# Gated linear attention with an MLP on one core: cosine from the absolute phase, six equal gate units, and a planner that knows a shared port and the order of the loads

## The chip, the cores and the metric

The program runs on one core of a Trainium2 chip. The metric is device time in microseconds (us) of one execution, lower is better. Engines are named as the profile names them: PE (TensorE, matrix products), DVE (VectorE), ACT (ScalarE, function tables), POOL (GpSimd) and SP, which here only issues loads and stores.

## The reference

Four batches, eight heads, 768 steps, 48 channels a head. A complex decay is applied at each step to a 48x48 state of each head; only the real part is read:

```python
mag = np.sqrt(a_re * a_re + a_im * a_im)
scale = np.minimum(mag, 0.999) / (mag + 1e-06)
for t in range(S):
    S_re, S_im = ar * S_re - ai * S_im + kv, ar * S_im + ai * S_re   # kv = k_t (x) v_t
    y[:, :, t] = einsum('bhd,bhde->bhe', q[:, :, t], S_re)
# x = y as [4, 768, 384]; then layer norm without bias, and
out = x + np.maximum(norm(x) * g_ln @ w_ch1, 0) @ w_ch2              # 384 -> 1536 -> 384
```

## The kernel before

The steps are cut into 24 chunks of 128, and the work goes in 12 **pairs** of two chunks, three pairs to a batch. A pair does this, with the planner's names for the steps:

- **Gates.** SP loads `are` and `aim` of the pair. ACT takes `ln` (into `w`) and `iv` (an exponential), DVE multiplies to `r` (the tangent of the phase step), `r2` is its square, ACT takes `u` (a logarithm), DVE makes the log magnitude `l`. PE sums `l` along the steps (`dec`), and ACT makes `e` and `en` from the sums. These ACT steps need the logarithm table.
- **Phase.** With the other table ACT takes the arctangent `th`, PE sums it along the steps (`ph`, in two PSUM banks, read back as 16-bit turns), DVE keeps the end for the next pair (`car`), ACT takes the sine of the phase (`sin`) and of half the phase (`sh`), and POOL or DVE makes the cosine from the latter, as 1 - 2 sh squared (`cos`, two instructions).
- **Attention.** `ke` and `qe` are k and q times the magnitudes, `ks` and `qs` those times cosine and sine (always DVE). PE transposes them, they are copied out of PSUM (`ksT`, `qsT`), PE forms the 128x128 scores (`am`), DVE masks them (`atm`), and PE forms `y`, with the state `G` carried by `gm`. `x` copies `y` out of PSUM.
- **MLP.** Statistics on DVE (`bn`), three transposes (`xtr`, `xT`), `mm1` with `relu` on ACT, `mm2`, and `ot` adds x. SP stores. The first layer's weights are folded once with the layer norm (`wp` on PE, `wc` copies).

Pairs are taken in **units** that share the table loads (`t_log`, `t_trig`) and the chunk decays (`tot`, `et`, `dps`, `decc`): `[[0], [1], [2, 3], [4, 5], [6, 7], [8, 9], [10, 11]]`.

No loop sets the order. Every step is put in a `Graph` with an engine, a cost, its needs and the ring buffers that it uses (k, q and `are` three deep, `vf` two). `Graph.order` is a list planner: at each turn it takes the engine that can start first, and among the steps ready within `SLACK` the one with the lowest key (a number of its group, plus its pair). A step with a second engine in `alt` goes where it would end first. The steps are then emitted in that order, and each engine runs its own in that order. The weights `w1r` and `w2b` are two DMAs issued by POOL (step `wl`), which convert to bf16 on the way; all other loads are SP's. The small constants (`one_b` to `cmat`) are made on POOL at the start.

Of the kernel before, what the change touches and what calls it, by code (L numbers as in the profile page):

```python
# [39 lines left out]
CHUNK = 0.196  # L40
SLACK = {"PE": 0, "ACT": 0.381, "DVE": 0.179, "POOL": 0.515, "SP": 0.565}
# [13 lines left out]
class Graph:  # L55
# [7 lines left out]
    def add(self, name, eng, cost, group, pos, emit, needs=(), uses=(), ps=None, alt=None, tail=0.0, c=0):  # L63
        assert name not in self.ops, name
        alts = {eng: (cost, tail)}
        if alt:
            alts[alt[0]] = (alt[1], tail)
        self.ops[name] = Op(name, alts, group, pos, emit, list(needs), list(uses), ps)
        self.ops[name].c = c

    def order(self, keys):
# [20 lines left out]
        dma_free = 0.0  # L92
# [9 lines left out]
        done = []  # L102
# [83 lines left out]
def kernel(  # L186
# [28 lines left out]
    UNITS = [[0], [1], [2, 3], [4, 5], [6, 7], [8, 9], [10, 11]]  # L215
# [46 lines left out]
    one_b = pool.tile([C, 1], FP32, name="one_b")  # L262
    half_n = pool.tile([C, R], FP32, name="half_n")
# [53 lines left out]
    for i, (f, cost) in enumerate(((c_one, .1), (c_ue, 1.6), (c_ue2, .5), (c_pick, 2.65),  # L317
                                   (c_ident, 1.85), (c_mask, 2.1), (c_sel, .6), (c_cmat, 5.0))):
# [11 lines left out]
    for i in range(2):  # L330
        g.add(("wl", i), "POOL", 1.4, "wl", i, lambda i=i: wl(i), tail=6.7)
# [8 lines left out]
    g.add(("wgc",), "DVE", .7, "wp", -1, wgc, needs=[("c_cmat",), ("gln",)])  # L340
    for jb in range(DF // 512):
        for ec in range(ND):
# [11 lines left out]
            g.add(("wc", jb, ec), "DVE", .6, "wc", jb * .1, wc, needs=[o], ps=(o, 1), alt=("ACT", .49))  # L354
# [14 lines left out]
    def pair_ops(P):  # L369
# [28 lines left out]
        def tt(name, **kw):  # L398
            engine(name).tensor_tensor(**kw)  # L399
# [25 lines left out]
        add(("l", P), "DVE", 1.27, f_l, needs=[("u", P)],  # L425
# [37 lines left out]
        if not last:  # L463
# [248 lines left out]
```

## Time and profile before

| | |
|---|---|
| time, median of 3 runs | 246.85 us (245.52 to 247.14) |
| the profiled execution's own time | 248.44 us |
| its span in the trace | 246.7 us |
| mean granted TensorE clock | 0.985 |
| DMA packets | 105671, 31.00 MB |

The span runs from the first to the last instruction; the 1.74 us beyond it are outside the trace. In the rows below a line such as L399 is a helper's line that many steps share, so steps are told apart by tile names. Buffer numbers are left out in the trace. The copies that write `w1b`, `ksT`, `qsT` share L358 (ACT) and L360 (DVE). The tile of `r2` is written as `r`.

### The profile page before, as it was taken

The numbers are of one execution on the slowest core, as the hardware profiler recorded it, in microseconds if no ns is written. First come the engines' busy times: TensorE is split into PE (matmuls) and PEld (weight loads), VectorE is DVE, ScalarE is ACT, GpSimd is POOL, SyncE is SP. The second block draws the span as 40 slices with busy tenths as digits, with TensorE's granted clock in tenths as the row PEclk, the third lists the DMA queues.
The fourth block names the chain that finished last, engine by engine and source line by source line (L and its number), as shares of the span: only waits on it lengthen the run. The fifth ranks groups of instructions, "written<-read, shape, count | busy, mean of one in ns | idle before, by whom it ended". The sixth has DMA issues, their size and how long they took to land. (4 is left out here: it accounts for less than half of the span.)

```text
span 246.7 us, 5275 instructions
## 1 busy us (share of the span) xinstructions
PE 198.2 (80%) x2123; PEld 147.2 (60%) x2123; DVE 192.3 (78%) x313; ACT 158.3 (64%) x193; POOL 104.0 (42%) x121
## 2 busy tenths in 40 slices
PE   0340087698896999989999878999698999999993
PEld 0020085247575867676677666696565887878762
DVE  0400669399999997999998998899999969996322
ACT  4260455598967769896694985599957857615320
POOL 8700321535966238583446670451675307301100
PEclk9999999799999999999999997999999999999999
DMA  7999898979984455928579044183421000001102
GB/s 194 251 205 196 189 210 170 201 175 291 185 186 111 130 159 112 201 73 192 162 139 217 32 115 111 32 160 100 92 69 35 33 3 35 0 35 35 64 32 96
DMA packets 105671, 31.00 MB, mean 126 GB/s; under 512 B 100656, under 2 KB 105264, under 8 KB 105648
## 3 DMA queue, kind: packets, MB, share of 16 engines
q1 hardware_dynamic: 103696, 28.32, 49.6%
q0 software_dynamic: 1952, 2.36, 5.5%
q8 instruction: 16, 0.26, 0.4%
q14 instruction: 7, 0.06, 0.1%
HBM read 28.31 MB, written 4.72 MB: 134 GB/s over the span
## 5 line engine op out<-in xcount | busy, mean ns | idle before, releaser
L623 PE MATMUL banks<-w2b,h 128*128 128x384 bf16 x288 | 55.6, 330 | 0.2 <-ACT h L614 0.2
L605 PE MATMUL banks<-xT,w1b 128*128 128x256 bf16 x432 | 53.2, 273 | 1.3 <-DVE xT L584 0.6
L605 PEld LDWEIGHTS <-w1b 128*128 128x128 bf16 x432 | 41.1, 98 | 8.7 <-DVE w1b L360 1.2
L614 ACT ACTIVATE h<-banks 128x1024 bf16<-128x1024 f32 x36 | 36.3, 1019 | 10.9 <-PE banks L605 10.8
L623 PEld LDWEIGHTS <-h 128*128 128x128 bf16 x288 | 26.4, 99 | 14.3 <-issue 1.4
L399 DVE TENSOR_TENSOR atm<-banks,mask 128x1024 bf16<-128x1024 f32 x24 | 28.6, 1214 | 3.1 <-PE banks L525 3.1
L507 PE MATMUL banks<-ident,ks 128*96 128x128 bf16 x192 | 14.3, 229 | 20.3 <-DVE ks L399 19.9
L399 POOL TENSOR_TENSOR r<-r 128x768 f16<-128x768 f16 x10 | 17.4, 1745 | 21.9 <-DVE r L399 21.9
L507 PEld LDWEIGHTS <-ks 128*96 128x96 bf16 x192 | 12.8, 129 | 23.1 <-DVE ks L399 22.8
L399 POOL TENSOR_TENSOR ke<-k,en 128x384 bf16<-128x384 f32 x13 | 14.1, 1101 | 27.2 <-ACT en L440 20.5
L569 ACT CAST x<-banks 128x384 bf16<-128x384 f32 x24 | 11.4, 478 | 19.0 <-PE banks L563 14.6
L629 DVE SCALAR_TENSOR_TENSOR ot<-banks,rstd,x 128x384 f32<-128x384 f32 x24 | 14.6, 609 | 10.5 <-PE banks L623 10.3
L476 POOL TENSOR_TENSOR sh<-sh 128x768 f16<-128x768 f16 x10 | 15.9, 1590 | 15.9 <-ACT sh L467 15.9
L399 DVE TENSOR_TENSOR qs<-qe,trig 128x768 bf16<-128x768 bf16 x24 | 21.7, 917 | 0.0
L399 POOL TENSOR_TENSOR qe<-q,e 128x384 bf16<-128x384 f32 x12 | 11.8, 988 | 20.3 <-DMA q<-in_q_dram 16.8
L399 DVE TENSOR_TENSOR ks<-ke,trig 128x768 bf16<-128x768 bf16 x24 | 19.3, 818 | 0.9 <-ACT trig L470 0.9
L435 PE MATMUL banks<-l,u_e 128*128 128x384 f16 x48 | 10.4, 342 | 11.7 <-DVE l L423 11.7
L591 POOL TENSOR_SCALAR rstd<-mv 128x2 f32<-128x2 f32 x12 | 3.4, 283 | 38.1 <-DVE mv L574 36.9
L643 ACT ACT_TABLE_LOAD x14 | 18.0, 1283 | 1.0 <-PEq L696 0.8
L507 PE MATMUL banks<-ident,qs 128*96 128x128 bf16 x192 | 14.2, 228 | 4.2 <-DVE ksT L360 2.3
L470 ACT ACTIVATE trig<-banks 128x768 bf16<-128x768 int16 x12 | 9.8, 816 | 10.6 <-DVE car L464 10.6
L454 PE MATMUL banks<-th,u_th 128*128 128x384 f16 x48 | 13.0, 357 | 4.0 <-ACT th L444 4.0
(78 smaller groups left out, 422.9 us busy)
## 6 DMA issues: line engine op xcount, KB each, us to landing
are<-in_a_re_dram SPq DMA_DIRECT2D x12, 384.0 KB, 3.5
aim<-in_a_im_dram SPq DMA_DIRECT2D x12, 384.0 KB, 4.3
k<-in_k_dram SPq DMA_DIRECT2D x24, 192.0 KB, 3.7
q<-in_q_dram SPq DMA_DIRECT2D x24, 192.0 KB, 3.8
vf<-in_v_dram SPq DMA_DIRECT2D x24, 192.0 KB, 3.6
out_dram<-ot SPq DMA_DIRECT2D x24, 192.0 KB, 1.9
w1r<-in_moe_w_ch_dram POOLq DMA_DIRECT2D x1, 1152.0 KB, 11.1
w2b<-in_moe_w_ch_dram POOLq DMA_DIRECT2D x1, 1152.0 KB, 17.9
```

The costliest lines, as they stand in the source:

```text
L399: engine(name).tensor_tensor(**kw)
L435: nc.tensor.matmul(heads(ps[:, c, 0:DM]), lhsT=u_e[:, c, j], rhs=step(T("l", P), j), start=(j == 0), stop=(j == R - 1))
L454: nc.tensor.matmul(heads(ps[:, c, 0:DM]), lhsT=u_th[:, c, j], rhs=step(T("th", P), j), start=False, stop=(j == R - 1))
L470: add(("sin", P), "ACT", .7, lambda: act(out=T("trig", P)[:, 1], in_=v16(), func=AF.Sin, scale=TWO_PI_SAFE / TURN), needs=[("ph", P)], use ...
L476: eng.tensor_tensor(out=T("sh", P), in0=T("sh", P), in1=T("sh", P), op=ALU.mult)
L507: nc.tensor.transpose(ps[:, h], T(nm, P)[:, c, h].rearrange("p a d -> p (a d)"), ident)
L569: add(("x", n), "ACT", .38, lambda n=n: nc.scalar.copy(out=T("x", n), in_=bank(("y", n))[:, 0:DM]), needs=[("y", n)], uses=[("x", n)], c=c ...
L605: nc.tensor.matmul(ps[:, jj], lhsT=w1b[:, dc, ts(gi * JG + jj, C)], rhs=T("xT", P)[:, dc].rearrange("p c t -> p (c t)"), start=(dc == 0), ...
L614: add(("relu", P, gi), "ACT", .91, lambda gi=gi, o=o: act(out=T("h", P)[:, ts(gi, JG)], in_=bank2(o).rearrange("p s (j t) -> p (s j) t", t ...
L623: nc.tensor.matmul(bank(("o", n))[:, 0:DM], lhsT=T("h", P)[:, j, ts(c, C)], rhs=w2b[:, j], start=(j == 0), stop=(j == NJ - 1))
L629: add(("ot", n), "DVE", .54, lambda n=n, c=c: nc.vector.scalar_tensor_tensor(out=T("ot", n), in0=bank(("o", n))[:, 0:DM], scalar=T("rstd", ...
L643: nc.scalar.preload_act_table_set({"log": "natural_log_exp_and_others", "trig": "trig_and_small"}[name])
```

## The change

The half-angle sine `sh` is replaced by the absolute value of the phase (`abs`, on DVE or ACT, written to the tile `sh`), and the cosine becomes one more ACT step, sin(pi/2 - |phase|), with a bias tile `quarter`. `r2` may run on ACT too, and `x` on DVE too. The first two units of one pair become one unit of two. The planner gets new keys, costs and slacks, a second condition for POOL and DVE steps that are marked `lock` (they don't overlap in its model), a model of how the POOL-issued loads push back the ones in flight, and the weight loads are added to the graph last.

```diff
-KEYS = {"ld_a": -10.982, "ld_qk": -2.438, "ld_v": -1.699, "vcast": 4.3, "t_log": -4.145, "ln":
...
+KEYS = {"const": -19.045, "ld_a": -3.747, "ld_qk": -2.454, "ld_v": -2.007, "vcast": 1.508,
...
+BIAS = {"abs": 0.134, "r2": -0.1, "ke": 0.052, "qe": 0.05, "kT": 0.179, "qT": -0.551, "wc": -1.356, "x": 0.12}
-SLACK = {"PE": 0, "ACT": 0.381, "DVE": 0.179, "POOL": 0.515, "SP": 0.565}
+SLACK = {"PE": 0, "ACT": 0, "DVE": 0, "POOL": 0, "SP": 0.478}
...
+                    if e in ("POOL", "DVE") and op.lock:
+                        t = max(t, lock_free)
...
+            if e in ("POOL", "DVE") and op.lock:
+                lock_free = t + cost
...
-            if tail:
+            if tail and e == "POOL":
+                for o, at in queued:
+                    if at > t:
+                        o.end += tail
+                dma_free = max(dma_free, t + cost) + tail
+                op.end = t + cost + tail + 1.8
+            elif tail:
+                queued.append((op, max(dma_free, t + cost)))
...
-    UNITS = [[0], [1], [2, 3], [4, 5], [6, 7], [8, 9], [10, 11]]
+    UNITS = [[0, 1], [2, 3], [4, 5], [6, 7], [8, 9], [10, 11]]
...
-        add(("r2", P), "POOL", 1.7, lambda: tt(("r2", P), out=flat(T("r2", P)), in0=flat(T("r", P)),
-                                               in1=flat(T("r", P)), op=ALU.mult),
-            needs=[("r", P)], uses=[("r", P), ("r2", P)], alt=("DVE", .48))
+        def f_r2():
+            if g.ops[("r2", P)].eng == "ACT":
+                act(out=flat(T("r2", P)), in_=flat(T("r", P)), func=AF.Square)
+            else:
+                tt(("r2", P), out=flat(T("r2", P)), in0=flat(T("r", P)), in1=flat(T("r", P)), op=ALU.mult)
+        add(("r2", P), "POOL", 1.7, f_r2, needs=[("r", P)], uses=[("r", P), ("r2", P)],
+            alt=[("DVE", .48), ("ACT", .74)], lock=True)
...
-        add(("sh", P), "ACT", .7, lambda: act(out=T("sh", P), in_=v16(), func=AF.Sin,
-                                               scale=TWO_PI_SAFE / TURN / 2),
-            needs=[("ph", P)], uses=[("sh", P)], key="sin", ps=(("ph", P), 2))
+        def f_abs():
+            if g.ops[("abs", P)].eng == "ACT":
+                act(out=T("sh", P), in_=v16(), func=AF.Abs)
+            else:
+                nc.vector.tensor_reduce(out=T("sh", P), in_=v16().unsqueeze(3), op=ALU.max,
+                                        axis=mybir.AxisListType.X, apply_absolute_value=True)
+        add(("abs", P), "DVE", .88, f_abs, alt=[("ACT", .7)], needs=[("ph", P)], uses=[("sh", P)], ps=(("ph", P), 2))
...
-        def f_cos():
-            eng = engine(("cos", P))
-            eng.tensor_tensor(out=T("sh", P), in0=T("sh", P), in1=T("sh", P), op=ALU.mult)
-            eng.tensor_scalar(out=T("trig", P)[:, 0], in0=T("sh", P), scalar1=-2.0, scalar2=1.0,
-                              op0=ALU.mult, op1=ALU.add)
-        add(("cos", P), "POOL", 2.5, f_cos, needs=[("sh", P)], uses=[("sh", P), ("trig", P)],
-            alt=("DVE", .9))
+        add(("cos", P), "ACT", .83, lambda: act(out=T("trig", P)[:, 0], in_=T("sh", P), func=AF.Sin,
+                                                scale=-TWO_PI_SAFE / TURN, bias=quarter),
+            needs=[("abs", P), ("c_one",)], uses=[("sh", P), ("trig", P)])
...
-            add(("x", n), "ACT", .38, lambda n=n: nc.scalar.copy(out=T("x", n), in_=bank(("y", n))[:, 0:DM]),
-                needs=[("y", n)], uses=[("x", n)], c=c, ps=(("y", n), 1))
+            add(("x", n), "ACT", .38, lambda n=n: put(("x", n), T("x", n), bank(("y", n))[:, 0:DM]),
+                alt=[("DVE", .47)], needs=[("y", n)], uses=[("x", n)], c=c, ps=(("y", n), 1))
```

What this makes of the instructions, counted over the whole program: on POOL the ten pairs of cosine instructions and ten of the `r2` squares go, and `ke`/`qe` rise from 25 to 30. On DVE come six `abs`, twelve `x` and five more `r2`; two cosines (two instructions each), six `w1b` copies, two copies of `ksT`/`qsT` in all and five `ke`/`qe` go. On ACT come twelve `cos`, five squares, six `w1b` copies and two `ksT`/`qsT` copies in all; six of the twelve `sh` passes stay as `abs`; twelve `x`, two table loads and one `et` go. PE loses sixteen small products.

POOL at the start, before: the two weight DMAs stand ahead of `sel` and `cmat`.

```order
masks.py:65 MEMSET mask 128x128
masks.py:66 AFFINE_SELECT mask<-mask 128x128
L326 DMA w1r<-in_moe_w_ch_dram 128x3x1536
L304 MEMSET sel 128x8
L307 MEMSET sel 64x1 x4
L308 MEMSET half_n 128x2
L328 DMA w2b<-in_moe_w_ch_dram 128x12x384
L311 MEMSET cmat 128x1152
L313 AFFINE_SELECT cmat<-cmat 128x384 x3
```

POOL at the start, now:

```order
masks.py:65 MEMSET mask 128x128
masks.py:66 AFFINE_SELECT mask<-mask 128x128
L323 MEMSET sel 128x8
L326 MEMSET sel 64x1 x4
L327 MEMSET half_n 128x2
L330 MEMSET cmat 128x1152
L332 AFFINE_SELECT cmat<-cmat 128x384 x3
L345 DMA w1r<-in_moe_w_ch_dram 128x3x1536
L347 DMA w2b<-in_moe_w_ch_dram 128x12x384
```

Both weight loads are issued after every constant. SP's loads at the start, before (`are_64` is the first ring buffer of `are`, and so on):

```order
L378 DMA are_64<-in_a_re_dram 128x8x96
L378 DMA aim_67<-in_a_im_dram 128x8x96
L378 DMA are_65<-in_a_re_dram 128x8x96
L378 DMA aim_68<-in_a_im_dram 128x8x96
L378 DMA are_66<-in_a_re_dram 128x8x96
L378 DMA aim_69<-in_a_im_dram 128x8x96
L383 DMA k_73<-in_k_dram 128x8x48
L383 DMA q_70<-in_q_dram 128x8x48
```

SP's loads at the start, now:

```order
L395 DMA are_65<-in_a_re_dram 128x8x96
L395 DMA aim_68<-in_a_im_dram 128x8x96
L400 DMA k_73<-in_k_dram 128x8x48
L400 DMA q_70<-in_q_dram 128x8x48
L400 DMA k_73<-in_k_dram 128x8x48
L400 DMA q_70<-in_q_dram 128x8x48
L404 DMA vf_76<-in_v_dram 128x8x48
L349 DMA gln<-in_moe_g_ln_dram 128x3x1
L404 DMA vf_76<-in_v_dram 128x8x48
L395 DMA are_66<-in_a_re_dram 128x8x96
```

The third pair's gates now stand behind the first pair's k, q and v. ACT's first phase, before: one pair's gates, the table, one pair's sines, and the other table.

```order
L440 ACTIVATE e_99<-banks 128x768
L643 ACT_TABLE_LOAD
L444 ACTIVATE th_92<-r_84 128x768
L467 ACTIVATE sh_106<-banks 128x768
L470 ACTIVATE trig_103<-banks 128x768
L643 ACT_TABLE_LOAD
L405 ACTIVATE w_83<-are_65 128x768
```

ACT's first phase, now (`trig_103` and `trig_104` are the first two pairs'):

```order
L684 ACTIVATE et_94<-banks 4x768
L663 ACT_TABLE_LOAD
L465 ACTIVATE th_92<-r_84 128x768
L465 ACTIVATE th_93<-r_85 128x768
L495 ACTIVATE trig_103<-banks 128x768
L498 ACTIVATE trig_103<-sh_106,quarter 128x768
L490 ACTIVATE sh_107<-banks 128x768
L495 ACTIVATE trig_104<-banks 128x768
L498 ACTIVATE trig_104<-sh_107,quarter 128x768
L663 ACT_TABLE_LOAD
```

Both pairs pass through one visit to each table; the first pair's `abs` is not in ACT's list, it stands in DVE's.

## Rows read from the trace of the kernel before

**Rows 1.** By stretch: length; busy PE, PEld, DVE, ACT, POOL; clock, DMA share, GB/s.
```profile
0.00:8.00 8.00, 0.00 (x0) 0.10 (x1) 1.81 (x3) 3.32 (x4) 6.80 (x27) 1.00 0.82 221
8.00:25.00 17.00, 5.16 (x20) 1.90 (x19) 1.67 (x3) 5.74 (x7) 2.89 (x4) 1.00 1.17 206
25.00:48.00 23.00, 12.58 (x118) 9.56 (x119) 15.31 (x30) 12.69 (x15) 6.42 (x8) 0.93 0.94 192
48.00:57.00 9.00, 7.82 (x44) 3.99 (x43) 8.94 (x13) 8.18 (x11) 5.07 (x4) 0.99 0.79 187
57.00:220.00 163.00, 149.65 (x1724) 114.69 (x1725) 153.79 (x244) 120.97 (x149) 80.94 (x77) 0.99 0.48 111
220.00:246.70 26.70, 23.03 (x224) 16.94 (x222) 10.83 (x23) 7.44 (x9) 1.84 (x4) 0.99 0.15 55
```

**Rows 2.** Timeline of the start: start, duration, instruction, [idle before it, releaser].
```profile
4.25 0.84 ACT L405 ACTIVATE w<-are 128x768 f32<-128x768 f32 x1 [2.18 <-DMA are<-in_a_re_dram]
...
5.11 1.00 POOL L326 DMA_DIRECT2D w1r<-in_moe_w_ch_dram  x1
...
6.90 1.06 POOL L328 DMA_DIRECT2D w2b<-in_moe_w_ch_dram  x1
6.94 6.65 SPq L383 DMA_DIRECT2D k<-in_k_dram  x1
...
9.10 1.87 POOL L313 TENSOR_SCALAR_AFFINE_SELECT cmat<-cmat 128x384 f16<-128x384 f16 x3
...
13.91 1.28 ACT L643 ACT_TABLE_LOAD   x1
...
17.90 0.81 ACT L467 ACTIVATE sh<-banks 128x768 f16<-128x768 int16 x1 [1.85 <-PE banks L454]
...
25.39 0.56 DVE L399 TENSOR_TENSOR ke<-k,en 128x384 bf16<-128x384 f32 x1 [11.13 <-DMA k<-in_k_dram]
...
31.89 1.94 PE L507 MATMUL banks<-ident,ks 128*96 128x128 bf16 x16 [14.03 <-DVE ks L399]
...
33.88 0.69 DVE L360 COPY ksT<-banks 96x1024 bf16<-96x1024 bf16 x1 [0.70 <-PE banks L507]
```

**Rows 3.** First two loads of `aim`, by tile, and time from issue to landing.
```profile
L378 SPq DMA_DIRECT2D aim<-in_a_im_dram x2: 567/858/1150, 1.3 to 3.0; - x2
...
DMA to landing us min/median/max: 4.1/4.6/5.2
```

**Rows 4.** First two loads of `k`, by tile, and time from issue to landing.
```profile
L383 SPq DMA_DIRECT2D k<-in_k_dram x2: 4139/5394/6648, 6.9 to 19.0; - x2
...
DMA to landing us min/median/max: 7.8/13.1/18.4
```

**Rows 5.** The page's DMA issues: size, us from issue to landing.
```profile
w2b<-in_moe_w_ch_dram POOLq DMA_DIRECT2D x1, 1152.0 KB, 17.9
```

**Rows 6.** The page's costliest groups: count, busy us, mean ns, idle before and releaser.
```profile
L399 DVE TENSOR_TENSOR atm<-banks,mask 128x1024 bf16<-128x1024 f32 x24 | 28.6, 1214 | 3.1 <-PE banks L525 3.1
...
L399 POOL TENSOR_TENSOR r<-r 128x768 f16<-128x768 f16 x10 | 17.4, 1745 | 21.9 <-DVE r L399 21.9
...
L569 ACT CAST x<-banks 128x384 bf16<-128x384 f32 x24 | 11.4, 478 | 19.0 <-PE banks L563 14.6
...
L476 POOL TENSOR_TENSOR sh<-sh 128x768 f16<-128x768 f16 x10 | 15.9, 1590 | 15.9 <-ACT sh L467 15.9
L399 DVE TENSOR_TENSOR qs<-qe,trig 128x768 bf16<-128x768 bf16 x24 | 21.7, 917 | 0.0
...
L399 DVE TENSOR_TENSOR ks<-ke,trig 128x768 bf16<-128x768 bf16 x24 | 19.3, 818 | 0.9 <-ACT trig L470 0.9
...
L470 ACT ACTIVATE trig<-banks 128x768 bf16<-128x768 int16 x12 | 9.8, 816 | 10.6 <-DVE car L464 10.6
```

**Rows 7.** Groups by form: the cosine's second instruction on POOL.
```profile
L477 POOL TENSOR_SCALAR trig<-sh 128x768 bf16<-128x768 f16 x10 | 9.6, 962 | 0.9
```

**Rows 8.** By tile: least, median and longest ns of `ks` on DVE.
```profile
L399 DVE TENSOR_TENSOR ks<-ke,trig x24: 526/568/1815, 28.8 to 212.0; 128x768 bf16<-128x768 bf16 x24
```

More of the change, by code (lines that the diff above doesn't have):

```diff
@@ L61, in __init__, with add @@
         self.bank = {}
-    def add(self, name, eng, cost, group, pos, emit, needs=(), uses=(), ps=None, alt=None, tail=0.0, c=0):
+    def add(self, name, eng, cost, group, pos, emit, needs=(), uses=(), ps=None, alt=None, tail=0.0, c=0, lock=False):
         assert name not in self.ops, name
         alts = {eng: (cost, tail)}
-        if alt:
-            alts[alt[0]] = (alt[1], tail)
+        for e, c_ in alt or ():
+            alts[e] = (c_, tail)
         self.ops[name] = Op(name, alts, group, pos, emit, list(needs), list(uses), ps)
         self.ops[name].c = c
+        self.ops[name].lock = lock
     def order(self, keys):
@@ L101, in order @@
                     ready[e].append(op)
-        done = []
+        done, queued = [], []
         def choose(n):
@@ L135, in order @@
                         t = max(t, b[0])
+                    if e in ("POOL", "DVE") and op.lock:
+                        t = max(t, lock_free)
                     if len(op.alts) > 1:
-                        other = [x for x in op.alts if x != e][0]
-                        if free[other] + op.alts[other][0] < t + op.alts[e][0] - 0.01:
+                        main = next(iter(op.alts))
+                        end = t + op.alts[e][0] + (BIAS[op.group] if e != main else 0.0)
+                        if any(max(free[x], t if x == "POOL" else 0.0) + op.alts[x][0]
+                               + (BIAS[op.group] if x != main else 0.0) < end - 0.01
+                               for x in op.alts if x != e):
                             continue
@@ L272, in c_one @@
         nc.gpsimd.memset(one_b, 1.0)
+        nc.gpsimd.memset(quarter, PI / 2)
     def c_ue():
@@ L338, in wgc @@
                                     scalar2=None, op0=ALU.mult)
-    g.add(("wgc",), "DVE", .7, "wp", -1, wgc, needs=[("c_cmat",), ("gln",)])
+    g.add(("wgc",), "DVE", .7, "wp", -.1, wgc, needs=[("c_cmat",), ("gln",)])
     for jb in range(DF // 512):
@@ L353 @@
             g.add(o, "PE", .66, "wp", jb * .1, wp, needs=[("wgc",), ("wl", 0)], ps=(o, 1))
-            g.add(("wc", jb, ec), "DVE", .6, "wc", jb * .1, wc, needs=[o], ps=(o, 1), alt=("ACT", .49))
+            g.add(("wc", jb, ec), "DVE", .6, "wc", jb * .1, wc, needs=[o], ps=(o, 1), alt=[("ACT", .49)])
     def put(name, dst, src):
@@ L424, in f_l @@
                                     scalar2=LNEPS, op0=ALU.min, op1=ALU.add)
-        add(("l", P), "DVE", 1.27, f_l, needs=[("u", P)],
+        add(("l", P), "DVE", 1.27, f_l, lock=True, needs=[("u", P)],
             uses=[("r2", P), ("w", P), ("l", P)])
@@ L511, in f_cp @@
                 put(name, T(dst, n), bank(o, D2).bitcast(BF16).rearrange("p (h t) -> p h t", h=H))
[L513 to L514 removed]
+            for nm, src, eng, alt in (("kT", "ks", ("DVE", .61), [("ACT", .91)]),
+                                      ("qT", "qs", ("ACT", .91), [("DVE", .61)])):
                 o = (nm, n)
@@ L593, in f_rstd @@
             nc.gpsimd.tensor_tensor(out=t, in0=t, in1=half_n, op=ALU.pow)
-        add(("rstd", P), "POOL", 1.0, f_rstd, needs=[("bn", P * R), ("bn", P * R + 1), ("c_sel",)],
+        add(("rstd", P), "POOL", 1.0, f_rstd, lock=True, needs=[("bn", P * R), ("bn", P * R + 1), ("c_sel",)],
             uses=[("mv", P), ("rstd", P)])
@@ L646 @@
     for ui, us in enumerate(UNITS):
-        before = [] if ui == 0 else [(nm, P) for P in UNITS[ui - 1] for nm in ("th", "sin", "sh")]
-        g.add(("t_log", ui), "ACT", 1.28, "t_log", us[0], lambda: table("log"), needs=before)
+        before = [] if ui == 0 else [(nm, P) for P in UNITS[ui - 1] for nm in ("th", "sin", "cos")]
+        g.add(("t_log", ui), "ACT", 1.3, "t_log", us[0], lambda: table("log"), needs=before)
         logs = [(nm, P) for P in us for nm in ("ln", "iv", "u", "e", "en")] + [("et", ui)]
-        g.add(("t_trig", ui), "ACT", 1.28, "t_trig", us[0], lambda: table("trig"), needs=logs)
+        g.add(("t_trig", ui), "ACT", 1.3, "t_trig", us[0], lambda: table("trig"), needs=logs)
         rows = 2 * len(us)
@@ L679 @@
             needs=[("dps", ui)], uses=[("dec", ui)], ps=(("dps", ui), 1))
+    for i in range(2):
+        g.add(("wl", i), "POOL", 1.4, "wl", i, lambda i=i: wl(i), tail=(6.2, 7.7)[i])
     for op in g.order(KEYS):
```

42 lines of the change are left out of this document (20 added, 22 removed), and 10 rows, old and new, of the table KEYS.

## Prediction

> **What bounds the kernel now.** I read the busy time by stretch first, since an average over the span hides the start. From 57 to 220 us PE is busy 149.65 of 163 us (92%) and DVE 153.79 (94%), so two engines are nearly full there and no single wait is worth much; ACT has 42 us idle and POOL half its time [rows 1]. After 220 us PE is busy 23.03 of 26.7: the last pairs' MLP. The start is different. In the 17 us from 8 to 25 PE is busy 5.16, DVE 1.67 and ACT 5.74, while the DMA engines are fully busy (share above 1) [rows 1]. The timeline says what is waited for. DVE stands idle 11.13 us until the first half of k lands, and `ke` starts at 25.39; PE gets its first transposes at 31.89 [rows 2]. That half of k was handed to the queue at 6.94, took 6.65 us to be accepted [rows 2] and landed 18.4 us after the start of its issue, at 25.3 [rows 4]. The second weight load, issued at 6.90 [rows 2], landed 17.9 us later, at 24.8 [rows 5]. Before the weights flowed, loads came fast: the second `aim`, issued at 3.04, landed 5.2 us later, at 8.2, and the first, issued at 1.29, at 5.4 [rows 3]: two 384 KB loads in 2.8 us, 1.4 each. So the weight loads, which nobody needs before the first layer's folding, starve the first k and q.
>
> **The start, step by step.** Weights: `sel` and `cmat` now stand ahead. The stretch from the end of the first weight issue, 6.11, to the end of `cmat`, 9.10 + 1.87 = 10.97, holds these constants and one weight issue of 1.06, so they take 3.8 us, and the first weight issue moves from 5.11 to about 9.0 [rows 2]. The old one began at 5.11 and the second `aim` still landed undisturbed at 8.2, so the squeeze begins some 3 us after the issue starts: now at about 12.
>
> Loads: two pairs' gates land by 8.2 as before. Then k, q, k, q of pair 0 instead of a third pair's gates. Once the weights were through, the first two halves of k landed at 25.3 and 18.96 + 7.8 = 26.8 with one q between [rows 4], 0.75 us apiece. Four of them are there by 8.2 + 4 x 0.75 = 11.2 at best, by 8.2 + 4 x 1.4 = 13.8 if each takes as long as a gate load; I take 12, because they are half the size. What comes behind them (v of pair 0, the third pair's gates) goes through the squeeze, which lasts as long as before and ends near 12 + 16.6 = 28.6 instead of 24.8. That v is needed only for `gm` and `y`, the gates only for the next unit.
>
> Gates of two pairs: before, the first load was used at 4.25 and the table switched at 13.91 [rows 2]. One pair more on ACT is five passes of about 0.84 (the `w` pass [rows 2]), 4.2 us; in series with DVE and PE as the first pair's were, it would be 9.66. Much of the second pair fits into ACT's waits for the first, but its `u` and `e` each queue behind one of them, so I take 5.1: table at 19.0. From the table to the first phase pass took 17.90 - 13.91 = 4.0, so the first `sin` is at 23.0. `sin`, `abs` and `cos` follow one another: 0.81, 0.91 and 0.81 to 25.5. (`abs` has no row; by columns it is 768/1024 of `atm`'s 1214 ns, 0.91, between `ks`'s least, 0.53 on the same columns, and `atm`'s 1.21, more columns and two inputs [rows 6, 8].) Sine and cosine products on two DVE halves, 0.55 each, put the first whole `qs` at 27.0, where PE had its first transposes at 31.89: 4.9 us earlier.
>
> Pair 1 gains more, because it no longer waits for a second round of both tables. I count by DVE, which then runs through. Before, DVE had done 1.81 + 1.67 + 15.31 + 8.94 = 27.73 us of work by 57.0 [rows 1]. In the changed list the work up to the second `xT` of pair 0 is 46 rows: 17 products and squares at 0.56 [rows 2], three `r` and three `l`, 7.1, two `atm`, 2.4 [rows 6], four copies at 0.69 [rows 2], `abs` and two `car`, 2.0, and small ones, 4.0: 27.8 us, as much. Of it 10.0 lies ahead of the first products of pair 0, so 17.8 follow from 25.3 on, and I add 1.6 of waits (the cold transposes, 1.94 for sixteen [rows 2], and `u` behind the weight copies on ACT): 44.7. **The lead is 57.0 - 44.7 = 12.3 us.** It counts only if loads keep up: by 57 us both kernels have moved the same bytes, since the DMA engines were busy all along (shares 0.94 and 0.79 from 25 to 57 [rows 1]).
>
> **The rest, step by step.** POOL loses 17.4 + 15.9 + 9.6 = 42.9 us of squares and cosines [rows 6, 7] and gains five products near 1.05, so of its 94.3 us after 25 us [rows 1] 40% go. This matters to DVE: `ks` takes 526 ns at least, 568 in the median, 1815 at worst [rows 8], 818 in the mean, `qs` 917 [rows 6]. Above the least that is 24 x 0.29 + 24 x 0.39 = 16.4 us; 40% less is 6.6 us saved.
> The Trainium skill, page "SBUF — State Buffer", section "SBUF: two separate sides", says that DVE and GpSimd share one port pair under an exclusive lock and that the loser fully blocks. The longest `ks` agrees; by that rule alone the whole 16.4 could go if nothing overlapped, which is the third case below.
>
> DVE gains six `abs`, 5.5 (3.2 to 7.3), twelve `x` at ACT's 0.48 [rows 6], 5.7, five squares at 0.53, 2.7; it loses six weight copies (0.64, by columns of `x`), 3.8, two cosines, 2.1, five `ke`/`qe` at 0.56, 2.8, two PSUM copies, 1.2: +4.0 net. DVE ends 2.6 us lighter (0.8 to 4.9). ACT: six passes more for the cosine (twelve `cos`, six `sh` gone), 4.9; five squares, 4.2; copies of weights and `ksT`/`qsT`, some 5; less twelve `x`, 5.7, two tables of 1.28 and an `et`: 5 us more, covered by its 42 us of idle time; without that cover they would cost 5. PE's sixteen small products cost nothing either way. PE has 163 - 149.65 = 13.35 us of idle time in the long stretch as a ceiling to any gain there, so DVE's 2.6 can be cashed; I take **2.6** (0 to 5). The last 26.7 us keep their form, mm1 and mm2 of the last pair.
>
> Sum: 12.3 + 2.6 = 14.9 us. The profiled run was 248.44 (span 246.7), which gives 233.5; against the median, 246.85, it is **232.0**.
>
> **Rivals.**
> *The squeeze catches pair 0 after all.* If the eighth load isn't through by 12, it lands when the weights are done, near 29, `qe` follows, and as that product stands in DVE's queue ahead of `abs`, the first products come at 31.0 instead of 25.3: 5.7 us of the lead go, 232.0 + 5.7 = 237.7. For it: the margin is under a microsecond, and SP was held 6.65 us by a full queue [rows 2]. Against: that hold began only when weights were flowing.
> The Trainium skill, page "DMA: Bandwidth & Descriptors", section "Queues, rings and completion order", says that each DMA engine takes turns between queues by packet; the k that took 18.4 us agrees, and by that rule weights don't wait for loads issued earlier.
>
> *The port relief is worth all of it.* With POOL's long instructions gone and the rest kept apart, DVE saves 16.4 - 4.0 = 12.4, within PE's 13.35: 246.85 - 12.3 - 12.4 = 222.2. Against: thirty POOL products remain, and PE is at 92% already.
>
> *The cosine stops ACT, slower.* In four units a `cos` on ACT waits for an `abs` that stands in DVE's queue, with `relu` behind it on ACT and PE behind that. `sin` already lost 10.6 us waiting for `car` on DVE [rows 6]. An `abs` behind two `atm` makes 2 x 1.21 + 0.91 = 3.3; six times 20 us: 232.0 + 20 = 252. It decides for slower from 14.9 / 6 = 2.5 us of stopped PE each. Against: PE has MLP work queued, and ACT is a quarter idle.
>
> *Given back.* The planner's new order leaves other gaps and the lead is spent by the end, 246: for it only that PE and DVE are both tight; nothing in the rows points to a place.
>
> **How the numbers follow.** Forecast 232.0, chance 0.50, its own range 228 to 236; squeeze 0.24 (238); full relief 0.10 (222); given back 0.07; slower 0.09. The range 225 to 241 holds the first two and part of the third, about 0.8. The three runs before lie within 0.7%, so about 1% (2.5 us) is what can be told from no change. Faster by more: 0.84; within: 0.07; slower: 0.09.
>
> **What would show it.** First transposes on PE near 27 us (31 by the first rival); first k landed by 12; the weights' issue at 9 and their landing near 29; DVE's cumulative 27.7 us reached near 45; `ks` and `qs` at a mean near 700 ns; POOL busy near 66 us; `abs` near 0.9 us; ACT near 163 us without long waits of `cos` for DVE. The prediction is wrong if the first products come at 27 us and the span doesn't follow, or if PE's idle time after the start grows beyond 13 us.

## The result and the profile after

The changed kernel takes 223.64 us (median of 4 runs, 222.67 to 224.57), the kernel before 246.83 beside it (245.52 to 247.14). The ratio is 0.9064, 95% interval 0.9011 to 0.9116: 23.1 us less. The forecast was 232.0, and the time lies below its range of 225 to 241. Below, ratios are turned into microseconds by 246.8.

By stretch, as in [rows 1] (length; busy PE, PEld, DVE, ACT, POOL; clock, DMA share, GB/s):

```profile
0.00:8.00 8.00, 0.00 (x0) 0.10 (x1) 1.81 (x3) 4.23 (x5) 6.73 (x28) 1.00 0.85 222
8.00:25.00 17.00, 7.55 (x28) 2.97 (x28) 8.15 (x14) 10.31 (x13) 2.78 (x4) 1.00 1.19 196
25.00:45.00 20.00, 18.14 (x182) 12.60 (x181) 19.30 (x36) 15.93 (x24) 8.20 (x7) 1.00 1.04 234
45.00:57.00 12.00, 11.93 (x138) 8.49 (x136) 11.23 (x20) 9.21 (x11) 6.73 (x9) 1.00 1.03 219
57.00:197.00 140.00, 134.40 (x1596) 106.64 (x1595) 129.03 (x235) 116.41 (x141) 38.24 (x50) 0.99 0.53 121
197.00:222.70 25.70, 22.05 (x181) 15.65 (x178) 7.38 (x13) 6.54 (x7) 0.92 (x2) 1.00 0.17 62
```

By 57 us DVE has now done 40.49 us of work, where [rows 1] add up to 27.73. After that PE leaves only 5.6 of 140 us idle.

The start, in the timeline, against [rows 2]:

```profile
8.72 1.00 POOL L345 DMA_DIRECT2D w1r<-in_moe_w_ch_dram  x1
9.73 1.06 POOL L347 DMA_DIRECT2D w2b<-in_moe_w_ch_dram  x1
...
18.25 1.28 ACT L663 ACT_TABLE_LOAD   x1
...
22.23 0.81 ACT L495 ACTIVATE trig<-banks 128x768 bf16<-128x768 int16 x1 [1.11 <-PE banks L475]
23.07 0.96 DVE L492 TENSOR_REDUCE sh<-banks 128x768 f16<-128x768 int16 x1 [3.77 <-ACT trig L495]
24.12 0.93 ACT L498 ACTIVATE trig<-sh,quarter 128x768 bf16<-128x768 f16 x1 [1.08 <-DVE sh L492]
24.66 0.56 DVE L416 TENSOR_TENSOR qs<-qe,trig 128x768 bf16<-128x768 bf16 x1
...
26.83 1.94 PE L527 MATMUL banks<-ident,qs 128*96 128x128 bf16 x16
```

Each of these steps stands within a microsecond of its forecast. Now the same amount of DVE's work marks the end of the start in both kernels: 27.7 us of it, reached at 43.4 after the change and at 57.1 before. Two stretches of each, first the kernel after:

```profile
0.00:43.40 43.40, 24.09 (x186) 14.14 (x187) 27.69 (x50) 29.41 (x39) 16.11 (x38) 1.00 1.06 217
43.40:222.70 179.30, 169.98 (x1932) 132.32 (x1929) 149.20 (x269) 133.22 (x159) 47.50 (x60) 0.99 0.51 120
```

and the kernel before:

```profile
0.00:57.10 57.10, 25.66 (x183) 15.65 (x183) 27.82 (x48) 30.02 (x36) 21.29 (x41) 0.97 0.97 200
57.10:246.70 189.60, 172.57 (x1943) 131.53 (x1942) 164.52 (x266) 128.31 (x158) 82.68 (x81) 0.99 0.43 103
```

So the start gives 13.7 us and what follows 10.3. Of these 10.3, PE has 2.6 us less work (172.57 to 169.98) and 7.7 us less idle time (17.0 to 9.3), and DVE ahead of it has 15.3 us less to do. Where that comes from shows in DVE's groups by form (count, busy us, mean ns, idle before):

```profile
L416 DVE TENSOR_TENSOR qs<-qe,trig 128x768 bf16<-128x768 bf16 x24 | 13.8, 596 | 1.2 <-ACT trig L495 0.9
...
L416 DVE TENSOR_TENSOR ks<-ke,trig 128x768 bf16<-128x768 bf16 x24 | 13.1, 564 | 0.1
...
L442 DVE SCALAR_TENSOR_TENSOR l<-r,w 128x768 f16<-128x768 f16 x12 | 11.9, 989 | 1.6 <-ACT r L437 1.6
...
L377 DVE CAST x<-banks 128x384 bf16<-128x384 f32 x12 | 6.6, 551 | 1.3 <-PE banks L583 1.2
L492 DVE TENSOR_REDUCE sh<-banks 128x768 f16<-128x768 int16 x6 | 5.7, 954 | 4.4 <-ACT trig L495 4.4
...
L416 DVE TENSOR_TENSOR r<-r 128x768 f16<-128x768 f16 x7 | 4.5, 639 | 0.1
```

`ks` and `qs` fell from 818 and 917 ns [rows 6] to 564 and 596: 41.0 us became 26.9, the same 48 instructions on the same tiles.

### The profile page after: what moved, and what is told of

The parts are those of the page before. It is cut to its first block, busy times and chain, and to the rows that moved or that the text cites. A ratio compares the mean times of both kernels' runs of the same rounds, so it can differ in the third digit from the quotient of the medians.

```text
span 222.7 us, 5217 instructions
## 1 busy us (share of the span) xinstructions
PE 194.1 (87%) x2115; PEld 146.5 (66%) x2115; DVE 176.9 (79%) x318; ACT 162.6 (73%) x197; POOL 63.6 (29%) x97
## 4 chain that ended last, share of the span: by engine, by line
PE 46%; DVE 26%; ACT 21%; issue 3%; DMA 2%; ACTq 0%; DVEq 0%
PE banks L643 14%; PE banks L625 12%; PE banks L527 5%; ACT h L634 3%; DVE atm L416 3%; PE banks L545 3%; ACT trig L495 3%; DVE r L416 3%; DVE qe L416 2%; PE banks L456 2%; PE banks L475 2%; ACT w L422 2%; ACT ksT L375 2%; ACT sh L490 2%; ACT L663 2%
## 5 line engine op out<-in xcount | busy, mean ns | idle before, releaser
L643 PE MATMUL banks<-w2b,h 128*128 128x384 bf16 x288 | 52.5, 326 | 0.4 <-DVE xT L604 0.4
L643 PEld LDWEIGHTS <-h 128*128 128x128 bf16 x288 | 26.8, 98 | 14.9 <-issue 0.5
L416 POOL TENSOR_TENSOR ke<-k,en 128x384 bf16<-128x384 f32 x17 | 17.6, 1048 | 37.4 <-ACT en L461 33.9
L456 PE MATMUL banks<-l,u_e 128*128 128x384 f16 x48 | 11.0, 356 | 13.7 <-DVE l L444 13.6
L407 POOL TENSOR_SCALAR v<-vf 128x768 bf16<-128x768 f32 x12 | 11.8, 986 | 33.6 <-DMA vf<-in_v_dram 19.3
L663 ACT ACT_TABLE_LOAD x12 | 15.4, 1283 | 1.0 <-PEq L719 0.8
L456 PEld LDWEIGHTS <-u_e 128*128 128x128 f16 x48 | 4.7, 103 | 17.3 <-issue 13.3
L545 PE MATMUL banks<-qsT,ksT 96*128 96x128 bf16 x192 | 14.7, 219 | 1.5 <-DVE ksT L377 1.0
L416 POOL TENSOR_TENSOR qe<-q,e 128x384 bf16<-128x384 f32 x13 | 12.8, 994 | 10.8 <-ACT e L461 10.8
L461 ACT ACTIVATE e<-banks 128x768 bf16<-128x768 f32 x12 | 9.7, 807 | 8.3 <-PE banks L456 7.7
L416 DVE TENSOR_TENSOR qs<-qe,trig 128x768 bf16<-128x768 bf16 x24 | 13.8, 596 | 1.2 <-ACT trig L495 0.9
L545 PEld LDWEIGHTS <-ksT 96*128 96x128 bf16 x192 | 11.8, 97 | 4.4 <-issue 1.5
L527 PEld LDWEIGHTS <-qs 128*96 128x96 bf16 x192 | 13.3, 129 | 1.5 <-DVE qs L416 0.8
L416 DVE TENSOR_TENSOR r<-aim,are 128x768 f16<-128x768 f32 x12 | 11.4, 948 | 3.7 <-ACT are L424 3.7
```

Source lines behind the costliest of these rows:

```text
L407: add(("v", P), "POOL", .82, lock=True, emit=lambda: nc.gpsimd.tensor_scalar(out=T("v", P), in0=T("vf", P), scalar1=1.0, scalar2=0.0, op0= ...
L456: nc.tensor.matmul(heads(ps[:, c, 0:DM]), lhsT=u_e[:, c, j], rhs=step(T("l", P), j), start=(j == 0), stop=(j == R - 1))
L461: add((nm, P), "ACT", .7, lambda nm=nm, sc=sc: act(out=T(nm, P), in_=bank2(("dec", P))[:, :, 0:DM], func=AF.Exp, scale=sc), needs=[("dec", ...
L527: nc.tensor.transpose(ps[:, h], T(nm, P)[:, c, h].rearrange("p a d -> p (a d)"), ident)
L545: nc.tensor.matmul(ps[:, h], lhsT=T("ksT", n)[:, h], rhs=T("qsT", n)[:, h], start=True, stop=True)
L643: nc.tensor.matmul(bank(("o", n))[:, 0:DM], lhsT=T("h", P)[:, j, ts(c, C)], rhs=w2b[:, j], start=(j == 0), stop=(j == NJ - 1))
```

## The experiments

Each time is set against the kernel before, run beside it. The first seven were made for two questions: what each part is worth alone, and why `ks` and `qs` became shorter.

**Loads' order alone** (kernel before, its order kept but for the moved steps):

```diff
+    seq = g.order(KEYS)
+    move(("wl", 0), ("c_cmat",)); move(("wl", 1), ("wl", 0))
+    move(("are", 2), ("vf", 0, 1)); move(("aim", 2), ("are", 2))
```

> The kernel before with one part of the change: the two weight loads issued behind the constants, and the third pair's gates loaded behind the first pair's v; nothing else moves. If the loads alone make the lead at the start: first transposes on PE near 21 us instead of 31.9, DVE's 27.7 us of work done near 48 instead of 57, time 237 to 239. If the lead needs the two-pair unit: pair 0 is early but pair 1 isn't, and the time is 242 to 246.

Measured: 237.5 us, ratio 0.9652 (0.9619 to 0.9685), 8.6 us. The timeline has the first transposes at 22.59:

```profile
22.59 1.94 PE L507 MATMUL banks<-ident,ks 128*96 128x128 bf16 x16 [4.93 <-DVE ks L399]
```

`k` landed 4.0 to 4.7 us after issue, DVE's 27.7 us came at 46.4, and `ks` and `qs` stayed at 817 and 917 ns. The load order (the weights' place and the third pair's gates together) makes a lead of 10.7 us by itself, with one pair a unit; 8.6 of it reach the end.

**Cosine alone**, with `abs` and `cos` both on ACT, directly behind `sin`:

```diff
-        eng.tensor_tensor(out=T("sh", P), in0=T("sh", P), in1=T("sh", P), op=ALU.mult)
-        eng.tensor_scalar(out=T("trig", P)[:, 0], in0=T("sh", P), scalar1=-2.0, scalar2=1.0, ...)
+        act(out=T("trig", P)[:, 0], in_=T("sh", P), func=AF.Sin, scale=-TWO_PI_SAFE / TURN, bias=quarter)
...
```

> The kernel before with one part of the change: the cosine as an ACT pass of the absolute phase (also ACT), order kept, so POOL loses its ten cosines (25.5 us) and DVE its two. If POOL's long instructions held up DVE (port theory): ks and qs fall from means of 818 and 917 to about 700, DVE busy from 192 to near 182, time 238 to 241. If the new order made the gain after the start (order theory): DVE falls by its two cosines alone, 2 us, time 245 to 248.

Measured: 240.81 us, 0.9794 (0.9754 to 0.9833), 5.1 us. The start is as before (27.7 us at 56.8); DVE has 183.1 us of work instead of 192.3:

```profile
L401 DVE TENSOR_TENSOR ks<-ke,trig 128x768 bf16<-128x768 bf16 x24 | 17.8, 755 | 0.9 <-ACT trig L471 0.9
L401 DVE TENSOR_TENSOR qs<-qe,trig 128x768 bf16<-128x768 bf16 x24 | 16.6, 704 | 0.0
```

Only two cosines were DVE's own (2.3 us). 6.6 us went from `ks` and `qs`, which the edit doesn't touch. The edit also takes POOL's two instructions (1.59 and 0.96 us) out of the way from the sine to `ks`; how the 5.1 us divide between that and DVE's lighter work this run doesn't tell.

**Both together**, the two edits above in one kernel:

> Both parts in the kernel before, order otherwise kept. Port theory and loads: the gains add, 228 to 232, and what is left to 223.6 is the squares, the units and the order. Order theory: as the loads alone, 237 to 246.

Measured: 235.27 us, 0.9552 (0.9513 to 0.9591), 11.1 us: the expected sum was missed, 8.6 and 5.1 don't add up. `qs` is at 704 ns, `ks` at 729, and DVE's 27.7 us come at 50.7, later than with the loads alone. Two ACT passes more stand in the start. But PE also ran slower there: four products of one shape took 1.49 us in this run (first line), 0.81 with the loads alone (second).

```profile
30.33 1.49 PE L437 MATMUL banks<-l,u_e 128*128 128x384 f16 x4
...
29.34 0.81 PE L435 MATMUL banks<-l,u_e 128*128 128x384 f16 x4
```

Which of the two costs how much is not told apart.

**Squares off POOL too** (the kernel with both; even pairs on DVE, odd ones on ACT):

```diff
+            if P % 2:
+                act(out=flat(T("r2", P)), in_=flat(T("r", P)), func=AF.Square)
+            else:
+                nc.vector.tensor_tensor(out=flat(T("r2", P)), in0=flat(T("r", P)), in1=flat(T("r", P)), op=ALU.mult)
```

> The kernel before with loads and cosine changed as in the run with both, and the squares taken off POOL as well, five more on DVE and six on ACT, order otherwise kept. Port theory: ks and qs fall to near 570, DVE to 177 to 180, time 229 to 232 against 235.3. Order theory: DVE rises by the squares' 3 us, time 234 to 237.

Measured: 231.74 us, 0.9382 (0.9338 to 0.9427), 15.3 us.

```profile
L401 DVE TENSOR_TENSOR qs<-qe,trig 128x768 bf16<-128x768 bf16 x24 | 16.1, 686 | 0.0
L401 DVE TENSOR_TENSOR ks<-ke,trig 128x768 bf16<-128x768 bf16 x24 | 13.5, 574 | 0.9 <-ACT trig L476 0.9
```

The cosine had held up mostly `qs`, the squares hold up `ks`. DVE does four squares more than in the run with both (six against two) and still has 4.3 us less work (182.7 to 178.4). From 57 to 197 us DVE is now as busy as in the changed kernel (128.46 and 129.03), so the 7.8 us that are still missing were lost earlier: by 57 us it has done 32.53 us of work, against 40.49. Pair 0 is even earlier here than in the changed kernel (transposes at 21.70 against 26.83); it is pair 1 that lags. Its first `qs` here, and then in the changed kernel:

```profile
54.36 1.29 DVE L401 TENSOR_TENSOR qs<-qe,trig 128x768 bf16<-128x768 bf16 x1
...
41.31 0.56 DVE L416 TENSOR_TENSOR qs<-qe,trig 128x768 bf16<-128x768 bf16 x1
```

Here pair 1 takes a round of both tables of its own (loads at 20.96 and 35.17 us).

**Weights early again**, in the changed kernel:

```diff
+    move(("wl", 0), ("c_mask",)); move(("wl", 1), ("c_sel",))
```

> The changed kernel with the two weight loads issued where they stood before, ahead of the constants on POOL; SP's order as changed. If the weights' place makes the lead: the first pair's k and q land between 14 and 26 us instead of by 12, first products near 28 instead of 24.7, time 226 to 229. If the order of SP's loads is enough: time 223 to 225.

Measured: 230.95 us, 0.9354 (0.9285 to 0.9423), 7.2 us above the changed kernel and above the expectation.

```profile
5.13 1.00 POOL L345 DMA_DIRECT2D w1r<-in_moe_w_ch_dram  x1
6.69 4.05 SPq L400 DMA_DIRECT2D k<-in_k_dram  x1
...
20.22 0.56 DVE L416 TENSOR_TENSOR qe<-q,e 128x384 bf16<-128x384 f32 x1 [8.11 <-DMA q<-in_q_dram]
...
34.08 1.90 PE L527 MATMUL banks<-ident,qs 128*96 128x128 bf16 x16
```

SP's queue is held again (4.05 us in one issue). The first pair's two `k`, one issued 0.83 us before the first weight load and one after it, land 10.6 and 16.5 us after issue, where they took 3.9 and 4.6 in the changed kernel. `qe` waits 8.11 us, and the first transposes come 7.2 us later than in the changed kernel: that is the whole loss.

**POOL given something to read, and something to write.** Twenty products of `cmat` with itself, behind the `v` and `rstd` of pairs 0 to 9 on POOL, into a tile that nothing uses; and as a control, in place of them, twenty memsets of `scratch` of nearly that length:

```diff
+        if op.name[0] in ("v", "rstd") and op.name[1] < 10:
+            nc.gpsimd.tensor_tensor(out=scratch[:, 0:2 * DM], in0=cmat[:, 0:2].rearrange("p c e -> p (c e)"),
+                                    in1=cmat[:, 0:2].rearrange("p c e -> p (c e)"), op=ALU.mult)
```

> The changed kernel with twenty extra products on POOL, one behind each v cast and each rstd of ten pairs: 768 columns of a constant times itself into a scratch tile that nobody reads, the shape of the squares that POOL lost, some 1.5 us each, no new wait. Port theory: they hold up DVE as the old squares and cosines did; before, 43 us of such POOL work went with 16 us or more of DVE's excess, so 30 us give DVE 8 to 12 us more, ks and qs means rise to 700 or more, and the time rises by 5 to 10 us. Order theory: DVE's work stays within 2 us and the time within 2 us.

> The same with memsets of 1536 columns into the scratch tile in place of the products, about 1.4 us each: POOL as long occupied, but reading nothing. If DVE is held up by POOL's reading: DVE within 2 us of the changed kernel, time within 2 us. If any POOL instruction does it, or the delay of POOL's own queue: as the products.

Measured: with the products 241.33 us, 0.9794 (0.9739 to 0.9848), 18.0 us above the changed kernel, and above the 5 to 10 that were expected. With the memsets 225.06 us, 0.9111 (0.9082 to 0.914), 1.2 us above it; the two intervals overlap. The groups with the products:

```profile
L708 POOL TENSOR_TENSOR scratch<-cmat 128x768 f16<-128x768 f16 x20 | 32.5, 1627 | 0.0
L416 DVE TENSOR_TENSOR ks<-ke,trig 128x768 bf16<-128x768 bf16 x24 | 19.5, 832 | 0.1
L416 DVE TENSOR_TENSOR qs<-qe,trig 128x768 bf16<-128x768 bf16 x24 | 18.1, 776 | 1.2 <-ACT trig L495 0.9
```

and with the memsets:

```profile
L708 POOL MEMSET scratch<- 128x1536 f16 x20 | 27.5, 1376 | 0.0
L416 DVE TENSOR_TENSOR qs<-qe,trig 128x768 bf16<-128x768 bf16 x24 | 14.1, 606 | 1.4 <-ACT trig L495 0.9 <-ACT trig L498 0.2
L416 DVE TENSOR_TENSOR ks<-ke,trig 128x768 bf16<-128x768 bf16 x24 | 13.8, 595 | 0.1
```

In the timeline one meeting of the two engines in each run, first with the products, then with the memsets:

```profile
93.75 1.76 POOL L708 TENSOR_TENSOR scratch<-cmat 128x768 f16<-128x768 f16 x1
94.11 1.82 DVE L416 TENSOR_TENSOR qs<-qe,trig 128x768 bf16<-128x768 bf16 x1
...
89.78 1.38 POOL L708 MEMSET scratch<- 128x1536 f16 x1
90.08 0.55 DVE L416 TENSOR_TENSOR qs<-qe,trig 128x768 bf16<-128x768 bf16 x1
```

A `qs` of 0.55 us that starts 0.36 us into POOL's 1.76 ends 0.42 after it: as if it had stood until POOL was nearly done. So it goes each time but one: of the nine `ks` and `qs` that begin beside a product, eight end 0.41 to 0.42 us behind its end, and the ninth takes 0.55 us. The fifteen that begin beside a memset take 0.54 to 0.56. POOL is nearly as busy with the memsets (90.9 us) as with the products (98.8), and DVE takes 178.0 against 191.4. So it is POOL's reading that holds DVE, not POOL's being busy, as far as a product and a memset differ in nothing else that matters; POOL's `v`, which reads one tile, holds DVE too (below). Some of the 18.0 us may be the clock's: from 57 to 197 us it was 0.96 against 0.99 in the changed kernel, and PE's work is 3.0 us longer in all (197.10 against 194.07), so up to some 3 us (an estimate). The Trainium skill, page "SBUF — State Buffer", section "Who interferes with whom", says just that of a DVE instruction with two inputs in SBUF: it contends with a GpSimd instruction that reads there, not with one that only writes. These two runs agree, 18.0 us against 1.2.

**What the rest of the start is made of.** Three ways in, of which two say little. First the changed kernel, replanned with the old units:

```diff
-    UNITS = [[0, 1], [2, 3], [4, 5], [6, 7], [8, 9], [10, 11]]
+    UNITS = [[0], [1], [2, 3], [4, 5], [6, 7], [8, 9], [10, 11]]
```

> The changed kernel with the old units, pairs 0 and 1 each alone, planned anew with the same keys. If the two-pair unit is part of the lead: one round of tables more, DVE's 27.7 us reached 3 to 5 us later than 43.4, time 226 to 229. If it isn't: 223 to 225.

Measured: 241.54 us, 0.9784 (0.9736 to 0.9831). The keys made for six units order seven badly: `gc` now stands on DVE ahead of `l` and waits for its load,

```profile
PE banks L364 <- DVE gc L354: 23.1, 1, 23.1
...
DVE gc L354 <- DMA gln<-in_moe_g_ln_dram: 15.8, 1, 15.8
```

so the run tells of that wait and not of the units. From the other end, the kernel with the squares, with the unit of pairs 0 and 1 (`UNITS` the other way round), ordered by the old keys:

> The kernel before with the loads' order, the cosine on ACT, the squares off POOL, and now also the first unit made of pairs 0 and 1 (that last is the one edit over the run with the squares, 231.74 us; the planner, with its old keys, orders the rest anew for it). By 57 us that run had 8 us less of DVE's work done than the changed kernel, and later both went at one rate. Units theory: the second round of both tables is what the start lacks, so this gives 223 to 227 us, with DVE's 27.7 us of work reached near 43 to 45. Order theory: what is left comes from the new keys, costs and engine choices, so this stays at 229 to 234 us, and DVE's 27.7 us is reached later than 46.

Measured: 248.11 us, 1.0052 (1.0021 to 1.0082), neither theory's number. Pair 1's `ke` stands on DVE ahead of pair 0's `qs`, and its `k` is loaded behind two more pairs' gates:

```profile
DVE ke L401 <- DMA k<-in_k_dram: 6.6, 1, 6.6
```

That is much like the first rival of the prediction, on the next pair: a unit of two pairs needs two pairs' k and q early. The next run was to mend it:

```diff
+    move(("gln",), ("vf", 0, 0))
+    last = ("aim", 2)
+    for n in (("k", 1, 0), ("q", 1, 0), ("k", 1, 1), ("q", 1, 1), ("vf", 1, 0), ("vf", 1, 1)):
+        move(n, last); last = n
+    move(("ke", 1, 0), ("r", 2)); move(("ln", 3), ("e", 2)); move(("iv", 3), ("ln", 3))
+    move(("r", 3), max((("iv", 3), ("ks", 1, 1)), key=lambda n: seq.index(name(n))))
```

> The kernel with the loads, the cosine, the squares and the unit of pairs 0 and 1, now with what came of the unit put in the changed kernel's order by hand: pair 1's k, q and v are loaded ahead of the fourth pair's gates, pair 1's ke stands on DVE behind pair 0's products and the third pair's r, and the fourth pair's ln, iv and r stand behind the third's e. In the run without that (248.1 us) DVE waited 6.6 us for pair 1's k, which stood in its queue ahead of pair 0's qs, and DVE's 27.7 us of work came at 56. Units theory: with the loads in step the unit gives what the start lacks, 223 to 228 us, DVE's 27.7 us at 43 to 46. Order theory: the unit itself gives little and the rest comes from the new keys and engine choices, 229 to 235 us.

Measured: 256.4 us, 1.0365 (1.0347 to 1.0382), and worthless: the fourth pair's squares were taken ahead of its `r`, and its `ln` read the buffer after the load that writes over it, so the kernel computes something else (and ACT waited 12.9 us for that load). With each step behind all that it needs:

> As the run before it, with the fourth pair's gates put in order rightly: there its squares were taken ahead of its r, and its ln read the buffer after the load of the seventh pair, for which ACT waited 12.9 us and DVE 14.8, so that its 256.4 us tell nothing of the unit. Here every step stands behind what it needs. Units theory: 223 to 228 us, DVE's 27.7 us at 43 to 46. Order theory: the unit itself gives little and the rest comes from the new keys and engine choices, 229 to 235 us.

Measured: 244.66 us, 0.9903 (0.9871 to 0.9935). Again outside both expectations: 12.9 us *slower* than with two units. The stretch from 25 to 45 us:

```profile
25.00:45.00 20.00, 12.97 (x104) 9.69 (x106) 15.50 (x27) 11.38 (x14) 7.54 (x8) 0.50 1.05 233
```

and the longest wait of PE behind DVE's and ACT's work, from 20 to 60 us:

```profile
PE banks L511 <- ACT w1b L360: 3.3, 1, 3.3
```

Pair 0 is as early as in the changed kernel (transposes at 26.51), but then a copy of weights holds PE for 3.3 us behind the fourth pair's gates on ACT, and pair 1's `qs`, at 41.31 and 43.25 in the changed kernel, stands at 56.27. And PE ran at the lower of its two clock levels (0.50, 1.2 GHz) through this whole stretch, where the run with the squares had 0.66 and the changed kernel was at the higher level from about 28.6 us on (its second sixteen transposes, at 28.56, take 1.14 us where the first took 1.94); if PE's 12.97 us here all scale with the clock, up to 6.5 us of them are the clock's (an estimate). So by the old keys the unit is a loss of 12.9 us, and what is the unit's in it, what the order's and what the clock's is not told apart.

**`x` on ACT again**, in the changed kernel's order:

```diff
+        if op.name[0] == "x":
+            op.eng = "ACT"
```

> The changed kernel in its order with all 24 x on ACT, as before the change. DVE loses 12 x of 0.55 us, 6.6 us, and ACT gains 12 of 0.48 us, 5.7 us. Since PE is busy 96% of the stretch from 57 to 197 us, neither should matter much: 222 to 226 us. If ACT's queue is what the change had to relieve, x waits behind relu and h on ACT and the time goes to 227 to 232 us; if DVE is still the bound after 57 us, it falls below 221.

Measured: 224.66 us, 0.9103 (0.9065 to 0.9142): no difference that can be told. DVE loses 5.6 us of work (171.3) and ACT gains 4.6 (167.2), without any gain in time: after the change DVE's length alone does not set the end.

**The planner without the lock condition**, all else as changed:

```diff
-                    if e in ("POOL", "DVE") and op.lock:
-                        t = max(t, lock_free)
```

> The changed kernel replanned without the condition that marked POOL and DVE steps don't overlap in the planner's model; keys, costs and slacks are the same. POOL has few long reading products left in either order. Theory that the removal of POOL's squares and cosines is the whole relief: ks and qs keep means near 560 to 620 ns and the time is 222 to 227 us. Theory that the condition keeps the two engines apart: ks and qs rise to 650 to 750 ns, DVE gains 4 to 9 us, and the time is 227 to 233 us.

Measured: 230.03 us, 0.9323 (0.9279 to 0.9367), 6.4 us above the changed kernel. But `ks` is at 575 ns and `qs` at 550, as short as with the condition, and DVE has 174.9 us of work. The time is the second theory's, the means are the first's: neither holds whole. What is longer is PE's stretch:

```profile
57.00:197.00 140.00, 130.56 (x1542) 102.19 (x1541) 126.37 (x225) 112.42 (x136) 48.38 (x55) 1.00 0.52 122
```

PE is busy 130.56 us there, against 134.40. Another order leaves other gaps; that the condition is worth 6 us because it keeps the engines apart isn't shown.

## Why the prediction was wrong

**Right: the start.** Weights at 8.72 (forecast 9.0), table at 18.25 (19.0), first `sin` 22.23 (23.0), first products 24.66 (25.3), transposes 26.83 (27.0), DVE's 27.7 us at 43.4 (44.7). The lead is 13.7 us where I had 12.3. The weights landed at 26.8 (near 29). That the transposes come within 0.2 us is chance: the products began 0.6 us early, and the second `qs` then took 1.18 us instead of 0.55, beside POOL's `v` (25.22 to 26.38). That the order of the loads is the lever is shown from both sides: 8.6 us gained with it alone (weights and third pair's gates), 7.2 us lost with the weights alone put back. How much of the lead the unit adds is not shown: in the old order the kernel with it is 12.9 us slower.

**Wrong: "40% less is 6.6 us saved".** That step scaled the excess of `ks` and `qs` by POOL's busy time. POOL's time did fall by 39% (103.96 to 63.61 us; forecast 66), but `ks` and `qs` lost 14.1 us, and their longest went from 1815 [rows 8] to 993 (`ks`). `l` lost 3.6 us more (13.4 and 6.4 to 11.9 and 4.3), and `ke` and `qe` 1.5, which I had not counted as held up at all. The excess doesn't follow POOL's busy time: twenty memsets add 27.5 us to POOL and 1.1 to DVE, twenty products add 32.5 and 14.5. It follows which POOL instructions stand beside a product of DVE, and the trace of the kernel before could have told me. Of its 48 `ks` and `qs`, twenty take over 0.7 us and hold 15.5 us of the excess, 16.0 above 0.535 us each. Every one of them ends 0.40 to 0.42 us behind a POOL instruction: sixteen, with 12.8 us, behind a square or a half of a cosine, two behind `v` and two behind `ke`. So 80% of the excess hung on the instructions that the change took out, where I put 40%. After the change three are left, all behind `v`. So "DVE ends 2.6 us lighter" became 15.4 (192.34 to 176.90). The other half of that sum was sound: DVE's additions were +4.0 by forecast and are +5.0 by the groups (squares 2.7, `abs` 5.7, `x` 6.6; less weight copies 3.8, cosines 2.3, `ke` and `qe` 2.8, PSUM copies 1.1).

**The size that followed.** I cashed 2.6 us of DVE's relief; the rest of the kernel gained 10.3. The ceiling of 13.35 us of PE's idle time that I named was a sound bound: 7.7 of it went, and PE's own work fell by 2.6, for which the prediction had nothing (why it fell is not shown).

**The rivals.** "The port relief is worth all of it" (222.2, chance 0.10) named the mechanism that ran, and its time is 1.4 us from the result; what I held against it, that thirty POOL products remain, weighs little: after the change none of them holds up a `ks` or `qs` by more than 0.1 us. The squeeze didn't catch pair 0: its `k` landed 3.9 and 4.6 us after issue. In the run with early weights it did, for 7.2 us (I had 5.7). That SP's 6.65 us were a full queue was my reading: the rows show a long issue, 4.05 us again with early weights, and not what held it. The cosine doesn't stop ACT: of all its waits for `abs`,

```profile
ACT trig L495 <- DVE sh L492: 1.7, 2, 1.0
ACT trig L498 <- DVE sh L492: 1.1, 1, 1.1
```

2.8 us in three waits are all, against the 20 of that rival. ACT's busy time is 162.63 (forecast 163), `abs` takes 954 ns (0.91 us). Nothing was given back.

**What makes up the 23.1 us.** Loads and cosine together 11.1, the squares 4.2, and 7.8 are left, lost in the first 57 us as DVE's work shows; there the unit of two pairs and the planner's new order came in. PE's clock may have a part in it: with the squares it was 0.66 from 25 to 45 us, so up to 5.2 of PE's 15.26 us there may be the clock's (an estimate), and the changed kernel was at the higher level for most of that stretch. What unit, order and clock are worth each stays open.

## What to carry to other kernels

If a DVE product has a wide spread (here 526 to 1815 ns on one shape), look up which instructions of POOL the slow ones end behind, and reckon with the excess that hangs on those that go (here 12.8 of 16.0 us), not with their share of POOL's time. A large transfer that is issued early (here two of 1152 KB) starves the small loads beside it, so it belongs behind the first loads that the pipeline waits for. And an order tuned to one structure says little about a changed structure: here three replanned kernels came out 6 to 18 us slower than those that they were made from.

## What the hardware showed that was not expected

Twenty POOL products of 1.63 us cost the kernel 18.0 us of its time, more than half of their own 32.5, though POOL is busy for only 41% of that span (98.8 of 239.5 us). A `ks` or `qs` that begins beside one ended 0.41 to 0.42 us behind it, in eight of nine cases.

And PE began at the lower of its two clock levels (1.2 and 2.4 GHz), before the change and after it, though the rows print a clock of 1.00 there ([rows 1] too). Four products of one shape tell it, in the changed kernel in a stretch that prints 1.00, then later in it, and in the kernel with the unit by the old keys in the stretch that prints 0.50:

```profile
10.03 1.44 PE L456 MATMUL banks<-l,u_e 128*128 128x384 f16 x4 [10.03 <-DVE l L444]
...
39.47 0.81 PE L456 MATMUL banks<-l,u_e 128*128 128x384 f16 x4 [0.45 <-DVE l L444]
...
39.32 1.49 PE L442 MATMUL banks<-l,u_e 128*128 128x384 f16 x4
```

By this sign PE reached the higher level near 28.6 us in the changed kernel and between 35.2 and 39.6 in the kernel before; with both edits it was still at the lower one at 37.65. In the kernel with the unit by the old keys it rose at 13.80, where the four products took 0.99 us, and was at the lower level again from 18.55 to 39.32. So a printed clock at the start of a trace is to be set against the length of a product before anything is read from it.
